# Cutting the first row tile's normalization in two pieces, ahead of its transposes

## The chip, the cores and the metric

One core of a Trainium2 chip. The metric is the device time of one execution in microseconds (us), as the median of several. The engines are TensorE (PE, with its weight loads as PEld), VectorE (DVE), ScalarE (ACT), GpSimd (POOL) and SyncE (SP), which issues most of the loads here. In this program TensorE's results go to the on-chip memory PSUM, and the other tiles lie in the on-chip memory SBUF.

## The reference, cut to what matters

```python
x = A_x                                   # 2048 rows of 640, bf16
xn = _layernorm(x, axis=-1)
s = _A_ref(xn, ...)                       # attention with 32 heads
g = _silu(_B_ref(xn, w_gate, w_up, w_down))
return x + s * g
# in _B_ref: sigmoid(xn @ w_gate) * (xn @ w_up), then @ w_down
```

Everything starts from the normalized rows `xn`. The kernel does `_B_ref` first, and so its first matmuls need `xn` of the first 512 rows, transposed.

## The kernel before

The first 512 rows are four row tiles of 128 rows ("tile 0" to "tile 3"). For each, VectorE takes statistics, ScalarE a square root, VectorE a reciprocal and the normalization; TensorE transposes five chunks of 128 columns into PSUM, and ScalarE copies them back to SBUF as the matmuls' moving operand (the one that is not loaded as weights). The engines run these instructions in the order of the program (in the trace tile 0's copies had their input at 5.70 us and started at 6.08 us, behind the square root at 5.87 us), so the order of these lines matters:

```python
load_x(0)
load_x(1)
for k in range(len(f_cuts) - 1):          # gate and up weights, piece by piece
    load_w(wg_sb, wg_r, k)
    load_w(wu_sb, wu_r, k)
    if k < 2:
        load_x(2 + k)                     # tiles 2 and 3 between the weights
# ... (cut)
def ln_apply(t):
    xn = xpool.tile([P, D], BF16, name="xn")
    nc.vector.tensor_scalar(
        xn[:], x_tiles[t], mv[:, t, 0:1], rstd[:, t, :],
        op0=ALU.subtract, op1=ALU.mult,
    )
    return xn
# ... (cut)
warm_up(NWARM[0])                         # nine filler matmuls
# ... (cut)
def turn(q):                              # five transposes, then the copies
    pT = pT_banks[:, q % 2, 0:NCD * P // 2].bitcast(BF16).rearrange("p (c n) -> p c n", c=NCD)
    for c in range(NCD):
        nc.tensor.transpose(pT[:, c, :], xn_t[q][:, c * P:(c + 1) * P], ident[:])
    for cs in ((slice(0, 2), slice(2, NCD)) if q == 0 else (slice(0, NCD),)):
        nc.scalar.activation(xnT[0][:, cs, q * P:(q + 1) * P], pT[:, cs, :], AF.Copy)

xn_t = {}
ln_stats(0)
ln_sqrt(0)
for q in range(TQ):
    if q + 1 < TQ:
        ln_part(q + 1, 0)                 # half the next tile's statistics
    nc.vector.reciprocal(rstd[:, q:q + 1, :], rstd[:, q:q + 1, :])
    xn_t[q] = ln_apply(q)
    if q + 1 < TQ:
        ln_stats(q + 1, 1)                # the other half
        ln_sqrt(q + 1)                    # ScalarE: ahead of tile q's copies
    if q == 0:
        turn(0)
        warm_up(NWARM[1])                 # two more fillers
        continue
    first_mm(q - 1, 0)                    # tile q-1's matmuls
    turn(q)
    first_mm(q - 1, 1)
    # ... (cut)
```

The softmax here doesn't subtract the row's maximum and nothing guards it: scores larger than these inputs give would overflow.

## Time and profile before

| | before |
|---|---|
| time, median of the first three runs (range) | 906.08 us (905.79 to 906.30) |
| span of the profiled execution | 904.4 us |
| VectorE's normalization of tile 0 starts | 4.75 us |
| VectorE waits for tile 2's load until | 6.34 us |
| TensorE starts tile 1's matmuls ("the release") | 8.99 us |

The release is the number to watch: ahead of it TensorE waits for ScalarE's copy of tile 1, and after it TensorE runs nearly without a gap (the profile's list of its waits has two more to the end, of 0.4 and 0.2 us).

### The profile page before, as it was taken

The numbers are of one execution on the slowest core, as the hardware profiler recorded it, in microseconds if no ns is written. First come the engines' busy times: TensorE is split into PE (matmuls) and PEld (weight loads), VectorE is DVE, ScalarE is ACT, GpSimd is POOL, SyncE is SP. The second block draws the span as 40 slices with busy tenths as digits, with TensorE's granted clock in tenths as the row PEclk, the third lists the DMA queues.
The fourth block names the chain that finished last, engine by engine and source line by source line (L and its number), as shares of the span: only waits on it lengthen the run. The fifth ranks groups of instructions, "written<-read, shape, count | busy, mean of one in ns | idle before, by whom it ended". The sixth has DMA issues, their size and how long they took to land.

```text
span 904.4 us, 18474 instructions
## 1 busy us (share of the span) xinstructions
PE 890.9 (99%) x7711; PEld 530.8 (59%) x7791; DVE 652.3 (72%) x1090; ACT 433.0 (48%) x511; POOL 179.3 (20%) x220
## 2 busy tenths in 40 slices
PE   8999999999999999999999999999999999999997
PEld 5545454556656565656565656565666666666664
DVE  4879956677677866785778677867786678666566
ACT  4323346764247533753375337643764285424240
POOL 0051212780001100110011001100110000002972
PEclk9999999999999999999999999999999999999999
DMA  9993374415544545364626362727293715264744
GB/s 280 271 265 95 97 146 104 119 54 87 86 91 68 135 78 99 60 143 69 109 60 143 62 115 52 151 54 123 36 167 50 126 34 117 48 111 147 155 120 114
DMA packets 188069, 100.38 MB, mean 111 GB/s; under 512 B 156176, under 2 KB 180368, under 8 KB 187984
## 3 DMA queue, kind: packets, MB, share of 16 engines
q1 hardware_dynamic: 159088, 57.85, 32.2%
q0 software_dynamic: 9408, 29.93, 14.0%
q10 hardware_dynamic: 19488, 11.41, 5.3%
q8 instruction: 61, 1.00, 0.5%
q14 instruction: 24, 0.20, 0.1%
HBM read 57.87 MB, written 5.24 MB: 70 GB/s over the span
## 4 chain that ended last, share of the span: by engine, by line
PE 96%; issue 1%; DVE 1%; DMA 1%; ACT 0%; SPq 0%; POOL 0%; DVEq 0%; POOLq 0%
PE ps_all L714 22%; PE ps_all L563 20%; PE ps_all L671 19%; PE ps_all L653 18%; PE ps_all L447 11%; PE ps_all L497 6%; PE ps_all L360 1%; DMA x_sb<-in_A_x_dram 0%; DVE qT L601 0%; ACT E L657 0%; DVE raw L221 0%; DMA out_dram<-o_sb 0%; POOL o_sb L726 0%; SPq L297 0%; DVE stats L324 0%
## 5 line engine op out<-in xcount | busy, mean ns | idle before, releaser
L657 ACT ACTIVATE E<-ps_all 128x1024 bf16<-128x1024 f32 x256 | 252.9, 1022 | 302.8 <-PE ps_all L653 255.5
L714 PE MATMUL ps_all<-wo_g,oT 128*128 128x128 bf16 (+2 forms) x1479 | 225.0, 295 | 3.3
L653 PE MATMUL ps_all<-qT,kT 64*128 64x512 bf16 x1536 | 194.4, 376 | 0.0
L671 PE MATMUL ps_all<-v_sb,E 128*128 128x193 bf16 x2048 | 189.8, 247 | 0.1
L671 PEld LDWEIGHTS <-E 128*128 128x128 bf16 x2048 | 168.6, 98 | 18.7 <-issue 6.8
L714 PEld LDWEIGHTS <-oT 128*128 128x128 bf16 x1542 | 121.5, 98 | 78.3 <-issue 2.1
L584 DVE COPY qp<-ps_all 128x512 f32<-128x512 f32 x150 | 100.7, 688 | 58.5 <-PE ps_all L563 58.4
L601 DVE TENSOR_TENSOR qT<-ps_all,qp 128x512 bf16<-128x512 f32 x165 | 109.6, 687 | 45.7 <-PE ps_all L563 37.4
L653 PEld LDWEIGHTS <-kT 64*128 64x128 bf16 x1536 | 75.3, 94 | 89.4 <-issue 5.2
L678 DVE TENSOR_TENSOR o_st<-ps_all,rden 128x768 bf16<-128x768 f32 x120 | 114.9, 957 | 5.0 <-DMA oT<-o_st 0.9
L202 POOL DMA_DIRECT2D raw<-in_A_wq_dram x80 | 48.5, 611 | 274.0 <-ACT wB L224 237.6
L135 POOL DMA_DIRECT2D k_sb<-in_A_k_cache_dram x32 | 32.7, 1027 | 276.3 <-DVE o_st L678 155.7
L219 ACT ACTIVATE raw<-raw,w_sc 128x1536 f16<-128x1536 bf16 x37 | 58.3, 1575 | 1.4 <-DMA raw<-in_A_wq_dram 0.5
L497 PE MATMUL ps_all<-wd_sb,hT_sb 128*128 128x128 bf16 (+1 forms) x377 | 52.4, 298 | 0.4
L563 PE MATMUL ps_all<-XA,wA 64*128 64x512 f16 x420 | 51.9, 376 | 0.2 <-DVE qp L584 0.2
L563 PE MATMUL ps_all<-XB,wB 64*128 64x512 f16 x420 | 52.0, 376 | 0.0
L563 PE MATMUL ps_all<-X,w 64*128 64x512 bf16 x420 | 51.9, 376 | 0.0
L749 DVE TENSOR_TENSOR acc_lo<-ps_all,acc_lo 128x640 f32<-128x640 f32 x48 | 39.4, 822 | 15.2 <-PE ps_all L714 15.1
L453 DVE TENSOR_TENSOR hT_sb<-ps_all,sig_sb 128x512 bf16<-128x512 f32 x48 | 32.4, 682 | 21.7 <-ACT sig_sb L452 11.4
L677 DVE RECIPROCAL rden<-ps_all 128x4 f32<-128x4 f32 x128 | 23.1, 180 | 33.5 <-PE ps_all L671 32.3
L452 ACT ACTIVATE sig_sb<-ps_all 128x512 bf16<-128x512 f32 x48 | 28.0, 596 | 39.8 <-PE ps_all L447 36.7
L749 DVE TENSOR_TENSOR acc_hi<-ps_all,acc_hi 128x640 f32<-128x640 f32 x48 | 39.3, 818 | 7.8 <-PE ps_all L714 7.8
(118 smaller groups left out, 761.6 us busy)
## 6 DMA issues: line engine op xcount, KB each, us to landing
raw<-in_A_wq_dram POOLq DMA_DIRECT2D x80, 192.0 KB, 3.8
k_sb<-in_A_k_cache_dram POOLq DMA_DIRECT2D x32, 192.0 KB, 5.9
wo_g<-in_A_wo_dram ACTq DMA_DIRECT2D x6, 960.0 KB, 6.8
v_sb<-in_A_v_cache_dram ACTq DMA_DIRECT2D x28, 192.0 KB, 3.7
gB_d<-gB_sb POOLq DMA_DIRECT2D x16, 160.0 KB, 4.2
gBa_sb<-gB_d SPq DMA_DIRECT2D x16, 160.0 KB, 3.8
xa_sb<-in_A_x_dram SPq DMA_DIRECT2D x16, 160.0 KB, 3.8
out_dram<-o_sb SPq DMA_DIRECT2D x15, 160.0 KB, 1.8
```

Of the source, the lines that this page charges most:

```text
L219: nc.scalar.activation(raw.bitcast(F16), raw, AF.Copy, scale=w_up)
L447: nc.tensor.matmul(gu[:, i, :], lhsT=w[:, c, f * P:(f + 1) * P], rhs=xnT[s][:, c, :], start=(c == 0), stop=(c == NCD - 1),)
L497: nc.tensor.matmul(oB_ps[:, d0:d0 + dsz], lhsT=hT_sb[:, f, q * P:(q + 1) * P], rhs=wd_sb[:, f, d0:d0 + dsz], start=(f == 0), stop=(f == NF ...
L563: nc.tensor.matmul(ps_all[:, b, :], lhsT=w(r, c), rhs=x[r, c, :], start=(first and k == 0), stop=(k == len(cs) - 1), skip_group_check=True,)
L584: nc.vector.tensor_copy(dst, part(b))
L601: nc.vector.tensor_tensor(q_out(i, u, pp), part(b), t, ALU.add)
L653: nc.tensor.matmul(ps[:, b, :], lhsT=kT[h, c * PC + j, :], rhs=qT_t[r][i, j][h, pp, :], start=(j == 0), stop=(j == PC - 1),)
L657: nc.scalar.activation(E_t[r, i, pp][:, c, :, :], ps, AF.Exp, scale=scale_qk)
L671: nc.tensor.matmul(o_ps[:, q // 2, q % 2, 0:DH + 1], lhsT=E[:, c, h, q * P:(q + 1) * P], rhs=vt[:, c, 0:DH + 1], start=(c == 0), stop=(c = ...
L678: nc.vector.tensor_tensor(o_st[:, :, h * DH:(h + 1) * DH].rearrange("p (b i) d -> p b i d", b=2), o_ps[:, :, :, 0:DH], rden[:].to_broadcas ...
L714: nc.tensor.matmul(oA[:, d0 - base:d0 - base + dsz], lhsT=oT_t[r, i, pp][:, q * PC + j, :], rhs=wo_t[runs[r][1]][:, cc, d0:d0 + dsz], star ...
L749: nc.vector.tensor_tensor(acc[t][:], oA[:, 0:D], acc[t][:], ALU.add)
```

## The change

The intent is that the transposes of tile 0's first two chunks start while the other three chunks are still being normalized. Only tile 0 is cut:

```diff
         def ln_apply(t):
             xn = xpool.tile([P, D], BF16, name="xn")
-            nc.vector.tensor_scalar(
-                xn[:], x_tiles[t], mv[:, t, 0:1], rstd[:, t, :],
-                op0=ALU.subtract, op1=ALU.mult,
-            )
+            cuts = [0, 2 * P, D] if t == 0 else [0, D]
+            for d in map(slice, cuts, cuts[1:]):
+                nc.vector.tensor_scalar(
+                    xn[:, d], x_tiles[t][:, d], mv[:, t, 0:1], rstd[:, t, :],
+                    op0=ALU.subtract, op1=ALU.mult,
+                )
             return xn
```

## The prediction

> **What bounds the kernel now.** I read the page first, for the whole span:
>
> ```profile
> span 904.4 us, 18474 instructions
> PE 890.9 (99%) x7711; PEld 530.8 (59%) x7791; DVE 652.3 (72%) x1090; ACT 433.0 (48%) x511; POOL 179.3 (20%) x220
> PE 96%; issue 1%; DVE 1%; DMA 1%; ACT 0%; SPq 0%; POOL 0%; DVEq 0%; POOLq 0%
> ```
>
> TensorE is busy for 99% of the span and holds 96% of the chain that ended last. All that the change can reach is in the remaining 13.5 us (904.4 - 890.9) in which TensorE has nothing, and of that only the part at the very start, where the first four row tiles are normalized and transposed. So the second view is the chain that ended last, in order of time, for the first microseconds:
>
> ```profile
> 2.71 3.61 DMA x_sb<-in_A_x_dram
> 6.32 0.02 issue
> 6.34 0.49 DVE stats L324
> 6.83 0.07 DVE rstd L383
> ...
> 7.81 0.22 DVE mv L329
> 8.03 0.02 issue
> 8.05 0.29 ACT rstd L366
> 8.35 0.60 ACT X L375
> 8.95 0.04 issue
> 8.99 0.72 PE ps_all L360 x10
> ```
>
> The columns are start, length, and what it was. This decides the case: from 8.99 us on the chain is TensorE's own work, and what releases TensorE at 8.99 is the copy of row tile 1 out of PSUM (L375). That copy goes back through the statistics of tile 2, which VectorE takes in between, to the landing of tile 2's load at 6.32 us. Nothing of tile 0's normalization, which the change cuts in two, is in the chain. A third view, the timeline of the same stretch, shows tile 0 itself:
>
> ```profile
> 4.75 0.45 DVE L337 TENSOR_SCALAR xn<-x_sb,mv,rstd 128x640 bf16<-128x640 bf16 x1
> 5.11 0.48 DVE L324 BATCH_NORM_STATS2 stats<-x_sb 128x6 f32<-128x320 bf16 x1
> 5.25 0.45 PE L373 MATMUL ps_all<-ident,xn 128*128 128x128 bf16 x5 [0.46 <-DVE xn L337]
> 5.63 0.21 DVE L329 BATCH_NORM_AGGREGATE mv<-stats 128x2 f32<-128x12 f32 x1
> 5.87 0.29 ACT L366 ACTIVATE rstd<-mv,eps_t 128x1 f32<-128x1 f32 x1 [1.36 <-DVE mv L329]
> 6.08 0.74 ACT L375 ACTIVATE X<-ps_all 128x256 bf16<-128x256 bf16 x2
> 6.34 0.49 DVE L324 BATCH_NORM_STATS2 stats<-x_sb 128x6 f32<-128x320 bf16 x1 [0.50 <-DMA x_sb<-in_A_x_dram]
> 6.49 0.71 PE L360 MATMUL ps_all<-X,wg_sb 128*128 128x128 bf16 x5 [0.35 <-ACT X L375]
> 8.25 0.68 ACT L375 ACTIVATE X<-ps_all 128x640 bf16<-128x640 bf16 x1
> 8.99 0.44 PE L360 MATMUL ps_all<-X,wg_sb 128*128 128x128 bf16 x5 [0.55 <-ACT X L375]
> ```
>
> TensorE did wait 0.46 us for tile 0's normalized row (the bracket at 5.25), and this is the wait that the change is meant to shorten. But the five transposes end at 5.70, and the copies that consume them start only at 6.08. In the program the square root for tile 1 (L366, 5.87) stands ahead of these copies on ScalarE, and it waits for tile 1's aggregate on VectorE (5.63 to 5.84).
>
> **What the Trainium skill says.**
> - "TensorE: Matmul & The Clock Gate", section "Architectural detail: the array is 16× 32×32, not 1× 128×128": the queues of ScalarE and VectorE are strict first-in first-out. The trace agrees: the copies sat ready, their input done at 5.70, and started after the square root at 5.87.
> - "VectorE: DVE Perf Modes", section "The TRN2 errata — SBUF-src ops pay a fixed extra latency per instruction": a large tile pays the fixed cost once, small tiles pay it each. The same page (section "The perf-mode tier table") has a 16-bit tensor_scalar in SBUF at four elements a cycle of 0.96 GHz. Two back-to-back instructions of L337 later in this trace take 0.80 us, so one starts 0.355 us (0.80 - 0.445) after the other; 640 / 4 / 0.96 is 0.167 us, which would leave 0.19 us fixed. No row of the trace has L337 at another size, so the split between stream and fixed cost isn't shown by it; at two elements a cycle the fixed part would be 0.02 us.
> - The TensorE page again, section "What's actually happening": the array's clock opens after some 3.4 us of activity, and the point moves from run to run. The trace has warm-up matmuls of 512 columns 0.42 us apart early on and 0.22 us apart from 5.54 us on, so it is fast by then.
>
> **The change part by part.**
>
> 1. Removed: one L337 over 128x640. Added: one over 128x256 (chunks 0 and 1) and one over 128x384 (chunks 2 to 4), for tile 0 alone. The elements are the same; one more instruction is paid. From the 0.19 and 0.02 us above, VectorE is later by an estimated **0.02 to 0.19 us**, most likely towards the upper end, as four a cycle is what the page gives.
>
> 2. Gained: the first piece lasts, at four a cycle, about 0.445 - 384/4/0.96 = 0.345 us and ends near 5.10 instead of 5.20 (at two a cycle 0.245 us, near 5.00). Transposes 0 and 1 start 0.10 to 0.20 us earlier. The second piece starts 0.255 us after the first and lasts 0.445 - 0.067 = 0.378 us: it ends near 5.38, so transposes 2 to 4 come 0.02 to 0.19 us **later** than today.
>
> 3. Moved with it: tile 1's second half of statistics (5.11), its aggregate (5.63), the square root (5.87) and therefore the two copies of tile 0 (6.08) all stand behind the added instruction, and slip by step 1's amount. The early transposes win nothing, as their copy waits for the square root: it had 0.38 us to spare already (6.08 - 5.70). Tile 0's first matmuls go from 6.49 to some 6.5 to 6.7. So on tile 0's own path the change is a loss of up to 0.19 us.
>
> 4. Whether it reaches the end. VectorE, after tile 1's aggregate at 5.84, idles 0.50 us until tile 2's load lands. A slip of 0.02 to 0.19 us fits inside, so from 6.34 on VectorE runs as before. The other route to 8.99 is TensorE: it does ten matmuls of tile 0, then tile 1's transposes at 7.43. If the ten start up to 0.19 us later, the transposes start at 7.6 at the latest and end by some 8.05; the copy they feed can't start before the square root of tile 2 at 8.05 in any case, and starts at 8.25. That still leaves 0.2 us. The ten further matmuls then end near 8.6, before 8.99.
>
> 5. The sum: 0.02 to 0.19 us lost before 6.3 us, absorbed by waits of 0.50 us on VectorE and 0.55 us on TensorE; **net 0.0 us**. Traffic, PSUM banks, tiles and the rest of the program are the same.
>
> **The rivals.**
>
> - *It helps as intended.* If the copies of tile 0 were released by the transposes, tile 0's first matmuls would come up to 0.2 us sooner. Against: ScalarE's order, and the bracket at 8.99, where TensorE waits anyway; it would only wait longer there. Even a full gain of 0.46 us, the whole wait, is 0.05% of 906 us. It would make 905.6 to 906.1.
> - *It hurts.* If the fixed cost were two or three times my estimate, or the load of tile 2 landed some 0.3 us sooner than in this trace, the slip would run past VectorE's 0.50 us and move 8.99 by perhaps 0.1 to 0.2 us: 906.2 to 906.3. For: the load's landing is not under the kernel's control. Against: it takes both, or a cost not seen in any row here.
> - *The clock.* The transposes and the two fillers after them shift by a tenth or two, and if TensorE's clock opened after 6.5 us in a run, the twenty-five matmuls and transposes before 8.99 would take twice their 0.055 us each, some 1.4 us more, of which half might show: 906.1 to 906.8. Against: the stretch is busier, not idler, and the kernel before runs the same risk.
>
> **Range and chances.** 906.08 us is the median of three runs from 905.79 to 906.30. I predict **906.1 us**, the same time. The range comes from the spread of runs and not from the change: half a microsecond of run spread, plus a few tenths for load landing and clock opening, gives **905.3 to 906.9**. 2% is 18 us, more than the whole 13.5 us that TensorE does not use, so faster by over 2% has a chance of 0.004; slower by over 2% needs a slow state or a fault, 0.004; within 2%, 0.992.
>
> **What would show each step.** (1) Tile 0's L337 in two rows, 128x256 and 128x384; the next statistics row starts later than 5.11 by 0.02 to 0.19 us, counted from the start of the normalization. (2) The wait of the first transpose falls from 0.46 us to 0.26 to 0.36 us. (3) The square root of tile 1 and the first copy of tile 0 are later by the same slip, and not earlier. (4) VectorE's wait for tile 2's load shrinks from 0.50 us by the slip while its end stays near 6.3, and the wait ahead of tile 1's matmuls, near 0.55 us, ends near 9.0. (5) The chain of waits still has the load and not tile 0. The prediction is wrong if the first copy of tile 0 starts earlier relative to the start of the normalization, if the row at 8.99 moves by more than the landing of the load explains, or if timed runs differ by more than their spread.

## The result, and the profile after

The changed kernel took **905.75 us** in the median (905.68 to 906.08, six runs), the kernel before 905.89 us (905.74 to 906.30, six runs). The ratio is 0.9998, with a 95% interval from 0.9985 to 1.0011: the same time. A ratio is the mean time of one kernel's runs over that of the other's runs of the same rounds, so it isn't quite the ratio of the medians.

The head of the page of the changed kernel:

```profile
span 904.0 us, 18555 instructions
PE 895.4 (99%) x7791; PEld 531.4 (59%) x7791; DVE 652.9 (72%) x1091; ACT 433.7 (48%) x511; POOL 179.0 (20%) x220
```

VectorE has one instruction more (1091 against 1090), as it should. TensorE's count is 7791 where the page before had 7711, though the weight loads are 7791 in both: the earlier trace had lost 80 matmul records. Its 890.9 us of busy time was therefore too low, and a count of PE that differs from that of PEld is how a reader notices.

The timeline of the changed kernel over the stretch that the prediction showed (start, length, engine, line, what; in brackets the idle time before it and what ended it):

```profile
4.77 0.64 DVE L339 TENSOR_SCALAR xn<-x_sb,mv,rstd 128x256 bf16<-128x256 bf16 x2
5.17 0.63 PE L375 MATMUL ps_all<-ident,xn 128*128 128x128 bf16 x5
5.32 0.49 DVE L324 BATCH_NORM_STATS2 stats<-x_sb 128x6 f32<-128x320 bf16 x1
5.97 0.44 DVE L324 BATCH_NORM_STATS2 stats<-x_sb 128x6 f32<-128x320 bf16 x1
6.08 0.30 ACT L368 ACTIVATE rstd<-mv,eps_t 128x1 f32<-128x1 f32 x1 [1.55 <-DVE mv L329]
6.29 0.75 ACT L377 ACTIVATE X<-ps_all 128x256 bf16<-128x256 bf16 x2
6.70 0.71 PE L362 MATMUL ps_all<-X,wg_sb 128*128 128x128 bf16 x5 [0.47 <-ACT X L377]
8.76 0.44 PE L362 MATMUL ps_all<-X,wg_sb 128*128 128x128 bf16 x5 [0.23 <-ACT X L377]
```

The transposes start 0.40 us after the normalization (5.17 - 4.77) where it was 0.50 us (5.25 - 4.75): a gain of 0.10 us. Tile 1's statistics start 0.55 us after it (5.32 - 4.77) where it was 0.36 us (5.11 - 4.75): a loss of 0.19 us. And the first copy and the first matmuls follow the loss, not the gain: 1.52 us after the normalization's start instead of 1.33 us, and 1.93 us instead of 1.74 us.

The fourth line is the one that the prediction did not have. Tile 2's load had already landed in this run: VectorE takes its statistics at 5.97 us with no bracket, so without any wait, where the kernel before waited until 6.34 us. That is why the release came at 8.76 us and not at 8.99 us. The last wait ahead of it was for TensorE: the copy of tile 1 started at 8.00 us, 0.26 us after the start of the square root before it (0.20 us in the kernel before), and 0.03 us after the end of tile 1's transposes (7.53 + 0.44). Those stand behind tile 0's copies and first matmuls. So with the early load tile 0 is on the path after all, by some 0.06 us.

### The profile page after: what moved, and what is told of

It reads as the page before. It is cut to its first block, busy times and chain, and to the rows that moved or that the text cites. A ratio compares the mean times of both kernels' runs of the same rounds, so it can differ in the third digit from the quotient of the medians.

```text
span 904.0 us, 18555 instructions
## 1 busy us (share of the span) xinstructions
PE 895.4 (99%) x7791; PEld 531.4 (59%) x7791; DVE 652.9 (72%) x1091; ACT 433.7 (48%) x511; POOL 179.0 (20%) x220
## 5 line engine op out<-in xcount | busy, mean ns | idle before, releaser
L716 PE MATMUL ps_all<-wo_g,oT 128*128 128x512 bf16 (+2 forms) x1542 | 228.3, 299 | 0.0
L499 PE MATMUL ps_all<-wd_sb,hT_sb 128*128 128x512 bf16 (+1 forms) x384 | 52.8, 299 | 0.0
```

The lines of the kernel that those rows point to most:

```text
L499: nc.tensor.matmul(oB_ps[:, d0:d0 + dsz], lhsT=hT_sb[:, f, q * P:(q + 1) * P], rhs=wd_sb[:, f, d0:d0 + dsz], start=(f == 0), stop=(f == NF ...
L716: nc.tensor.matmul(oA[:, d0 - base:d0 - base + dsz], lhsT=oT_t[r, i, pp][:, q * PC + j, :], rhs=wo_t[runs[r][1]][:, cc, d0:d0 + dsz], star ...
```

## The experiments

**Theory A.** The cut costs VectorE one instruction's fixed time, about 0.19 us, and brings nothing, as the copies stand behind VectorE's work on tile 1; the cost hides behind the landing of tile 2's load when that is late. What reaches the end is the release, one for one. **Rivals:** the cut itself brought the load forward (B); a delay at the start is made up later (C); only the order on ScalarE keeps the cut from paying (D); and the clock of TensorE, where the prediction had put it as a risk.

Twelve runs in all, in three groups, each group on one chip with the kernel before run beside it: 905.99 us in the first (905.87 to 906.42), 906.16 us in the second (905.76 to 906.71), 906.13 us in the third (905.50 to 906.46). All timed runs were in the fast state; before_again, after_again and early_cut_again are single runs, whose state is unknown.

### Does the cut move the load, or does the load move by itself?

Both kernels once more, unchanged.

> The kernel before, once more, to see how far the landing of row tile 2's load moves by itself. Theory A (the load of tile 2 sets the release of TensorE before tile 1's matmuls, and lands where it likes): the landing of tile 2's load differs by some tenths from 6.3 us, and the release near 8.99 us moves with it, down to about 8.55 us at the earliest, where VectorE's own chain takes over. Rival B (the cut itself brought the load of tile 2 forward in the changed kernel): landing at 6.3 again, within 0.1 us, and the release at 9.0.

> The changed kernel once more. Theory A: tile 2's load lands anywhere from 5.9 to 6.4 us; the release is at the later of 8.76 us (VectorE's chain with the cut in it) and the landing plus 2.65 us. Rival B: landing below 6.0 us and release at 8.76 us again.

The kernel before took 905.73 us, its statistics of tile 2 waited until 6.20 us, only 0.14 us less than in its first trace, and its release came at 8.86 us. The changed kernel took 906.15 us; the timeline of this second trace of it has

```profile
6.49 0.49 DVE L324 BATCH_NORM_STATS2 stats<-x_sb 128x6 f32<-128x320 bf16 x1 [0.47 <-DMA x_sb<-in_A_x_dram]
9.14 0.27 PE L362 MATMUL ps_all<-X,wg_sb 128*128 128x128 bf16 x2 [0.55 <-ACT X L377]
```

The changed kernel had the early landing once (5.97 us or before) and the late one once (6.49 us). Rival B falls: the cut does not force the early landing, and without the cut the load ended VectorE's wait anywhere from 6.05 us (in copyfirst_whole, below) to 6.50 us (in skip0). That the earliest landing of all came with the cut may be chance; the traces are too few to say. When the load is late, the release is 2.65 or 2.66 us behind it in both kernels (8.99 - 6.34, 8.86 - 6.20, 9.14 - 6.49), and the cut's 0.19 us is gone in the 0.47 us of waiting.

### How much does one more piece cost, and does a delay reach the end?

Tile 0 in five pieces, and in twenty.

```diff
-            cuts = [0, 2 * P, D] if t == 0 else [0, D]
+            cuts = list(range(0, D + 1, P)) if t == 0 else [0, D]        # cut5
+            cuts = list(range(0, D + 1, P // 4)) if t == 0 else [0, D]   # cut20
```

> Tile 0 in 5 pieces of 128 columns, one per transpose: four added instructions, 0.76 to 0.84 us of VectorE. Theory A: the slack of 0 to 0.5 us eats part of it, release at 9.3 to 9.4 us, the whole time 0.3 to 0.8 us longer (906.3 to 906.6). Rival C: within 0.1 us of the kernel before.

> Tile 0 normalized in 20 pieces of 32 columns: 19 added instructions. By the cost read from the changed kernel (0.19 to 0.21 us for one more), VectorE is 3.6 to 4.0 us later. Theory A (a start-up cost above the slack of about 0.5 us reaches the end one for one): release of TensorE near 12.0 to 12.6 us and the whole time longer by 3.0 to 3.8 us, about 909.3. Rival C (a delay at the start is made up later, as TensorE waits elsewhere): less than 1 us longer.

The timelines of the two (cut5 first) show the pieces, and then where tile 1's statistics start:

```profile
4.78 1.21 DVE L339 TENSOR_SCALAR xn<-x_sb,mv,rstd 128x128 bf16<-128x128 bf16 x5
5.90 0.49 DVE L324 BATCH_NORM_STATS2 stats<-x_sb 128x6 f32<-128x320 bf16 x1
```

```profile
4.81 4.05 DVE L339 TENSOR_SCALAR xn<-x_sb,mv,rstd 128x32 bf16<-128x32 bf16 x20
8.78 0.48 DVE L324 BATCH_NORM_STATS2 stats<-x_sb 128x6 f32<-128x320 bf16 x1
12.40 0.74 PE L362 MATMUL ps_all<-X,wu_sb 128*128 128x128 bf16 x5
12.94 0.50 PE L362 MATMUL ps_all<-X,wg_sb 128*128 128x128 bf16 x5
```

From the start of the normalization to tile 1's statistics it takes 0.36 us whole, 0.55 us in two pieces, 1.12 us in five (5.90 - 4.78) and 3.97 us in twenty (8.78 - 4.81). That is 0.19 us for each added piece, three times over: 0.19 / 1, 0.76 / 4, 3.61 / 19. One size from another gives the rest: pieces of 128 columns are 1.12 / 5 = 0.224 us apart and pieces of 32 are 3.97 / 20 = 0.198 us apart, so 96 columns take 0.026 us, four columns in 1.1 ns. A piece is a fixed 0.19 us plus its columns.

In cut20 the release came at 12.94 us, some 4 us late, and the time was 910.45 us (909.76 to 911.12), 4.29 us longer. So a delay at the start is not made up later, and rival C falls. It was expected to be 3.0 to 3.8 us: the release was later than VectorE's 3.6 us explain. By VectorE alone it would have come near 12.2 us, an estimate: tile 2's statistics at 9.42 us, plus the 2.79 us from there to the release in the changed kernel's first trace. But TensorE ran at half its rate until about 13 us (the group of five matmuls at 12.40 us is followed by the next after 0.54 us; from 13.28 us on it is 0.28 us), and the copy of tile 1 waited 0.63 us for its transposes. The granted clock, the share of full speed that the profile records for TensorE, reads 1.00 in this stretch (9 to 13 us), so here the distance between matmuls shows the slow clock and that record does not. In cut5 the release came at 9.34 us, as expected, but the time was 906.39 us (906.07 to 906.46), only 0.23 us longer, with overlapping ranges. The expected 0.3 to 0.8 us was too much; at this size the runs do not tell a difference.

### Is it only ScalarE's order?

Tile 1's square root behind tile 0's copies, with and without the cut.

```diff
             if q + 1 < TQ:
                 ln_stats(q + 1, 1)
-                ln_sqrt(q + 1)
+                if q > 0:
+                    ln_sqrt(q + 1)
             if q == 0:
                 turn(0)
+                ln_sqrt(1)
```

> The changed kernel with tile 1's square root put behind tile 0's copies on ScalarE. Theory A: the copies now follow the transposes, first copy near 5.5 instead of 6.29 us, tile 0's first matmuls near 5.9 instead of 6.70 us; yet TensorE is released for tile 1's matmuls where it was, 8.76 to 8.99 us, as that goes by the load and VectorE: same time within 0.15 us. Rival D (the order on ScalarE alone kept the change from paying): 0.3 us or more faster than the kernel before.

> The same order on ScalarE, tile 0 in one piece. Theory A: first copy near 5.6 us, tile 0's matmuls near 6.0 us, release as before, same time within 0.15 us. What the cut alone brings where nothing else stands ahead of the copies is the difference of the first copy's start in this run and in copyfirst_cut: expected 0 to 0.1 us in favour of the cut.

With the cut 906.16 us (906.02 to 906.69), whole 906.14 us (906.11 to 906.64): both as the kernel before (906.16 us). These times could not show the 0.3 us that rival D expects (the intervals of the ratios reach from 0.9987 to 1.0013, over 1 us to each side); the traces have to. The releases came at 9.22 and 8.96 us, where the kernel before has 8.99 and 8.86 us. The timelines, with the cut and then whole, show why, and a miss of mine:

```profile
5.15 0.79 PE L375 MATMUL ps_all<-ident,xn 128*128 128x128 bf16 x5
5.98 0.77 ACT L377 ACTIVATE X<-ps_all 128x256 bf16<-128x256 bf16 x2 [1.46 <-PE ps_all L375]
6.96 0.16 DVE L385 RECIPROCAL rstd<-rstd 128x1 f32<-128x1 f32 x1 [0.36 <-ACT rstd L368]
```

```profile
5.22 0.45 PE L373 MATMUL ps_all<-ident,xn 128*128 128x128 bf16 x5
5.71 0.77 ACT L375 ACTIVATE X<-ps_all 128x256 bf16<-128x256 bf16 x2 [1.22 <-PE ps_all L373]
```

I had expected the first copy near 5.5 us with the cut, as it needs chunks 0 and 1 only. It started 0.04 us after the end of the **last** transpose in both (5.15 + 0.79 and 5.98; 5.22 + 0.45 and 5.71). The listing of the built program says the same: of tile 0's two copies, the first waits for TensorE and the second for nothing, so the first one's wait covers all five transposes. (The count that it waits for there is 14: nine fillers and five transposes.)

```
L377 Activation X<-ps_all 128x2x128 [waits PE]
L377 Activation X<-ps_all 128x3x128
```

So early transposes of two chunks have no taker, with either order, and rival D falls on this. (A copy that waits for two transposes only was not tried.) And the cut makes the last transpose later: in the changed kernel it ends at 5.80 us (5.17 + 0.63), 1.03 us after the normalization's start, against 0.95 us (5.70 - 4.75) before. With the copies free to go first, the whole tile had its first copy 0.99 us after the normalization's start (5.71 - 4.72) and the cut one 1.23 us (5.98 - 4.75), where I had expected a gain of 0 to 0.1 us. About 0.16 us of that is TensorE's clock, slow in the one trace (transposes of 0.79 us against 0.63 us). In this trace the transposes also follow the fillers with no idle time between: here the slow clock left no wait to shorten.

The new order has a cost of its own, which the expectations had not counted. Tile 1's square root now comes after tile 0's copies, at 6.63 us with the cut and 6.37 us whole instead of 6.08 and 5.87 us, and VectorE's reciprocal waits for it (the bracket at 6.96 us). The releases are 2.26 and 2.27 us behind that reciprocal, and not 2.65 us behind the load, which had landed by 6.10 and at 6.05 us. So this pair shows that the copies cannot use the early chunks. It does not show that the load holds the release in this order: in copyfirst_whole the chain that ended last goes back from the release through this square root to tile 0's copies and transposes.

### What is the most that tile 0 can give?

Tile 0 goes to its transposes as loaded.

```diff
-            xn_t[q] = ln_apply(q)
+            xn_t[q] = ln_apply(q) if q > 0 else x_tiles[0]
```

> A wrong result on purpose: tile 0 goes to its transposes as loaded, its normalization is left out, so that nothing of it is left to shorten. It is more than any cut could win. Theory A: tile 0's transposes near 4.8 to 5.0 us, its first matmuls near 6.1 us, but the release for tile 1's matmuls stays where tile 2's load puts it (8.8 to 9.1 us), and the time within 0.25 us of the kernel before. Rival (tile 0 is on the path): 0.3 us faster or more.

It took 905.91 us (905.51 to 906.42) beside 906.13 us, ratio 1.000 with an interval from 0.9987 to 1.0012: no gain shows when all of tile 0's normalization is left out. The interval is over 1 us wide to each side, so by the times alone the rival's 0.3 us is not excluded; the trace says more. Its timeline:

```profile
5.16 0.74 PE L373 MATMUL ps_all<-ident,x_sb 128*128 128x128 bf16 x5
6.50 0.49 DVE L324 BATCH_NORM_STATS2 stats<-x_sb 128x6 f32<-128x320 bf16 x1 [0.81 <-DMA x_sb<-in_A_x_dram]
9.15 0.44 PE L360 MATMUL ps_all<-X,wg_sb 128*128 128x128 bf16 x5 [0.55 <-ACT X L375]
```

VectorE waits 0.81 us for tile 2's load instead of 0.50 us, and the release is 2.65 us behind the load again. So with a late load nothing is gained from tile 0. For an early one there is no trace of this run, and it says nothing. The transposes came at 5.16 us and not at the expected 4.8 to 5.0 us: they stand behind the nine fillers, and this run's clock was slow and its tile 0 landed 0.3 us later than in the traces above. The first matmuls followed at 6.54 us and not near 6.1 us.

### Without the load to hide behind

Two attempts. The first loads tiles 2 and 3 at once from ScalarE's queue. (The hunk that gives `load_x` the queue's engine as a second argument is left out.)

```diff
         load_x(1)
+        load_x(2, nc.scalar)
+        load_x(3, nc.scalar)
         for k in range(len(f_cuts) - 1):
             load_w(wg_sb, wg_r, k)
             load_w(wu_sb, wu_r, k)
-            if k < 2:
-                load_x(2 + k)
```

> Row tiles 2 and 3 loaded at once from ScalarE's queue, tile 0 normalized in one piece: the wait for the load is gone, VectorE runs without idle time. Theory A: VectorE takes tile 2's statistics straight after tile 1's aggregate at 5.85, TensorE is released near 8.5 us instead of 8.76 to 8.99, and the whole time falls by 0.2 to 0.5 us, to about 905.5. If the extra load delays row tile 0's landing, all of it shifts by that.

> The same with the cut of the change. Theory A: with no wait on VectorE to hide in, the cut's 0.21 us shows in full: the release of TensorE for tile 1's matmuls is 0.2 us later than in early_whole, and the time about 0.2 us longer (0.02%). Rival (the early transposes do help): release at the same time or earlier than in early_whole.

Whole: 905.51 us in the median, but one of five at 907.39 us. With the cut: 907.24 us, with one run at 906.15 us and four from 907.07 to 907.53 us. Tile 0 itself landed late (its statistics start at 3.69 and 3.61 us instead of 3.06 us), and the two traces differ little: releases at 9.18 us and 9.30 us. From the same first instruction, tile 0's statistics, that is 5.49 us and 5.69 us, so the cut's 0.2 us does show, as expected. The time was expected to be 0.2 us longer, too, and that was missed: the cut's 0.2 us does not explain 1.7 us between the medians. (Against the kernel before, the ratio is 1.0011 with an interval from 0.9999 to 1.0024, which counts as the same.) So the cut kernel was run again for a trace of a long run.

> early_cut once more, for a trace of its longer times (four of its five runs took 907.07 to 907.53 us, and its trace was of the 906.15 us one). Theory: TensorE's clock. With row tile 0 landing 0.6 us later, TensorE stands idle for 0.3 to 1.0 us ahead of the transposes, and in the longer runs the matmuls of the first tiles still go at half rate, five in 0.53 us instead of 0.28 us, up to some 10 us or later. If this run is a short one, or a longer one with matmuls at 0.28 us, the theory isn't shown.

It took 907.42 us, a long one. Busy time by stretch (start:end, length, then busy time and count for PE, PEld, DVE, ACT, POOL, then the granted clock, DMA share and GB/s), for this run and then for the 906.15 us run of the same kernel:

```profile
4.70:8.10 3.40, 1.92 (x14) 0.78 (x13) 3.25 (x12) 1.24 (x4) 0.00 (x0) 1.00 1.27 234
8.10:11.40 3.30, 3.30 (x35) 3.30 (x34) 2.63 (x9) 1.29 (x3) 0.00 (x0) 0.52 1.11 302
```

```profile
4.70:8.10 3.40, 2.48 (x20) 1.12 (x19) 3.25 (x12) 1.24 (x4) 0.00 (x0) 1.00 1.28 233
8.10:11.40 3.30, 3.07 (x56) 2.95 (x54) 2.33 (x8) 1.97 (x4) 0.00 (x0) 1.00 1.10 308
```

The granted clock falls to 0.52 from about 8.1 to 11.4 us, TensorE does 35 matmuls there instead of 56, the release comes at 10.17 us, and the span is 905.6 us against 904.4 us. In the stretch before, it had been busy for 1.92 us of 3.40 us against 2.48 us. The release is 0.87 us later (10.17 - 9.30). Of that, 0.34 us is tile 0's still later landing (3.95 - 3.61); the other 0.53 us goes with the slow clock, as the copy of tile 1 waited 0.43 us for its transposes there. That the idle time brought the slow clock on is argued from these two traces, not shown, and the other long runs have no trace. Whether the cut makes the long runs more frequent (four of five against one of five) is open.

The second attempt is gentler: only tile 2's load goes ahead of the first weights.

```diff
         load_x(1)
+        load_x(2)
         for k in range(len(f_cuts) - 1):
             load_w(wg_sb, wg_r, k)
             load_w(wu_sb, wu_r, k)
-            if k < 2:
-                load_x(2 + k)
+            if k == 1:
+                load_x(3)
```

> Row tile 2 loaded ahead of the first weights instead of behind them, tile 0 in one piece. In early_whole the added loads held up tile 0's own landing by 0.6 us; here they should not. Theory A: VectorE no longer waits for tile 2 and takes its statistics near 5.95 us; TensorE is released for tile 1's matmuls near 8.55 us (8.86 and 8.99 us in the two traces of the kernel before); the whole time 0.3 us shorter at most, about 905.7 to 906.0.

> The same with tile 0 cut in two. Theory A: nothing to hide in, so the cut's 0.19 us on VectorE shows in the release: near 8.75 us, 0.2 us later than in x2first_whole; the whole time 0.1 to 0.3 us longer than there. Rival (the early transposes pay once the load is out of the way): release no later than in x2first_whole.

The timelines, whole and then cut: tile 2's statistics and the release.

```profile
5.72 0.44 DVE L325 BATCH_NORM_STATS2 stats<-x_sb 128x6 f32<-128x320 bf16 x1
8.52 0.44 PE L361 MATMUL ps_all<-X,wg_sb 128*128 128x128 bf16 x5 [0.23 <-ACT X L376]
```

```profile
5.90 0.44 DVE L325 BATCH_NORM_STATS2 stats<-x_sb 128x6 f32<-128x320 bf16 x1
8.69 0.44 PE L363 MATMUL ps_all<-X,wg_sb 128*128 128x128 bf16 x5 [0.23 <-ACT X L378]
```

The wait for tile 2's load is gone, and the cut now costs 0.17 to 0.18 us where it can be seen: 5.90 against 5.72 us, and 8.69 against 8.52 us at the release, close to the expected 0.2 us. The rival, that early transposes pay once the load is out of the way, falls. But the whole times went the other way: 905.81 us whole (905.71 to 905.83) and 905.59 us cut (905.47 to 905.97). The expected 0.1 to 0.3 us in disfavour of the cut was missed; the ranges overlap, so the runs show no difference either way. Tile 3's load is next to bind: VectorE waited for it until 8.12 us in the one trace and 8.40 us in the other, and tile 2's transposes moved with that (9.22 and 9.50 us). Both versions are 0.3 to 0.5 us below the kernel before in the median, but their ratios (0.9998 and 0.9997, intervals from 0.9984 to 1.0012 and 1.0009) do not tell them from it.

### The release and the span

| run | release, us | span, us | difference |
|---|---|---|---|
| before, first and second trace | 8.99, 8.86 | 904.4, 904.0 | 895.4, 895.1 |
| changed, first and second trace | 8.76, 9.14 | 904.0, 904.4 | 895.2, 895.3 |
| skip0 | 9.15 | 904.6 | 895.5 |
| cut5 | 9.34 | 904.4 | 895.1 |
| cut20 | 12.94 | 908.7 | 895.8 |
| copyfirst whole, cut | 8.96, 9.22 | 904.4, 904.9 | 895.4, 895.7 |
| x2first whole, cut | 8.52, 8.69 | 903.9, 904.1 | 895.4, 895.4 |
| early whole, cut, cut again | 9.18, 9.30, 10.17 | 903.9, 904.4, 905.6 | 894.7, 895.1, 895.4 |

What follows the release takes 894.7 to 895.8 us, whatever came ahead of it, while the release moves over 4.4 us (8.52 to 12.94). The start is worth what it does to the release, and the rest of the kernel scatters by more than the cut costs.

## Why the prediction was right

Time and range held: 905.75 us against 906.1 us predicted, in 905.3 to 906.9 us. That alone is cheap: the rivals' times, from 905.6 to 906.8 us, lie in the same range, and even leaving tile 0's normalization out gave 905.91 us. The steps are confirmed or not by the traces.

1. **The cost of one more piece** (step 1) was put at 0.02 to 0.19 us, likely towards the upper end. It is 0.19 us, and the split behind it, 0.19 us fixed plus four columns a cycle, held for pieces of 640, 128 and 32 columns.
2. **The gain** (step 2): the first piece lasts 0.348 us, predicted 0.345 us, and the second 0.377 us, predicted 0.378 us. The first transposes are 0.10 us sooner, the lower end of 0.10 to 0.20 us. Its sign, an idle time of 0.26 to 0.36 us ahead of them, can't be read: in this trace the fillers ran until 5.02 us instead of 4.79 us.
3. **The copies slip instead of gaining** (step 3): 0.19 us later, square root and first matmuls with them. The reason given, ScalarE's order, was true but not the whole of it: the copy waits for all five transposes, so it could not have gained with any order.
4. **Absorbed by VectorE's wait for tile 2's load** (steps 4 and 5): right in the second trace of the changed kernel, with 0.47 us of waiting left, and not in its first. There the load had landed before 5.97 us, nothing absorbed the slip, and the release at 8.76 us came from the chain that the cut lengthens. By the 0.19 us that the cut adds, it would have been near 8.57 us without it (an estimate; x2first_whole and x2first_cut show the pair, 8.52 and 8.69 us). Step 4 also gave the route over TensorE 0.2 us to spare; in this trace that route was the last by some 0.06 us. That the release still came earlier than in the kernel before was luck with the load. The prediction had this as its second rival but named the load's place in one trace as if it were fixed; it moves by half a microsecond. "The chain still has the load and not tile 0", its fifth sign, failed in that trace. The sum changed by 0.19 us of 906 us.
5. **The room in TensorE** (first part) was put at 13.5 us from 890.9 us of busy time. That figure lacked 80 matmul records; with all of them the room is 8.6 us (904.0 - 895.4). It only made the 2% more remote.
6. **The clock** was named as a rival for both kernels. It cost nothing visible in the four traces of these two, but it delayed the release in early_cut_again and in cut20.

## What to carry to other kernels

Before cutting an operation so that its first part can be used early, look for the instruction that would use it, what else stands ahead of it on its engine, and whether its wait covers the first part alone or everything; here all three were against the cut. A cut in this vector instruction cost a fixed 0.19 us per piece, from 640 columns down to 32, and in a start-up chain that time lands on the next tile. When a wait ends with a transfer, take a second trace before calling it the bound: its landing moved by more than the change was worth.

## What the Trainium skill lacked or had wrong

- "VectorE: DVE Perf Modes", section "The TRN2 errata — SBUF-src ops pay a fixed extra latency per instruction", has a fixed 58 cycles in its table and says that about 150 were measured, which is 0.06 and 0.16 us at its 0.96 GHz, for the duration of one instruction (a copy, where it measured). A tensor_scalar with two per-partition scalars lasted a fixed 0.28 us plus its columns here (0.445, 0.310 and 0.287 us for 640, 128 and 32 columns), and from start to start the fixed part was 0.19 us (0.36, 0.224 and 0.198 us). Its four elements a cycle hold.
- "TensorE: Matmul & The Clock Gate", section "What's actually happening", has the clock fall back after at least one idle window of about 3.4 us, and does not say how much work a window may hold and still count as idle. In early_cut_again it fell to 0.52 for about 3.3 us after a stretch in which TensorE had been busy 1.92 us of 3.40 us by the profile; in early_cut, with 2.48 us of 3.40 us, it did not fall. Where the windows lay isn't known, and two traces make no threshold.
- "DMA: Bandwidth & Descriptors", section "Latency and other measured facts", gives an HBM latency of 0.2 us on average and 2 us at high load, but no page that I read says how far the landing of one load scatters from run to run. The load of tile 2 in these two kernels, issued at 2.7 us, ended VectorE's wait at 6.34, 6.20 and 6.49 us and was there by 5.97 us in another run.
